# Emptying PSUM banks through ScalarE and adding them to the output by accumulating DMAs, instead of adding on VectorE

## The chip, the cores and the metric

The kernel runs on one core of one Trainium2 chip. The metric is the device time of one execution in microseconds (us), as the median of several runs. Engines are named as in the profile: PE is TensorE (PEld its weight loads), DVE is VectorE, ACT is ScalarE, POOL is GpSimd and SP is SyncE.

## The reference

The input x is 2048 rows of 576 numbers in float32. All is float32.

```python
xn = layernorm(x)                       # over the 576 columns, eps 1e-5
out = x + A(xn, wqkv, wo) + B(xn, w1, w2)

# A: attention, 32 heads of 18; row s sees rows s, s-2, ..., s-14 (masked below 0)
q, k, v = split(xn @ wqkv)              # wqkv 576 x 1728
A = softmax(q . k[s - 2j] / sqrt(18)) @ v[s - 2j], heads joined, @ wo   # wo 576 x 576

# B: a dense layer with relu
B = relu(xn @ w1) @ w2                  # w1 576 x 4608, w2 4608 x 576
```

## The kernel before

The rows are split by parity into two phases (`ph`, `NPH` = 2), since the attention's stride of 2 never mixes them. A phase has eight row tiles of 128 rows (`NI`), which B takes in pairs, four groups (`tb`) of 256 rows. The 4608 inner columns of B are 36 blocks of 128, taken in 12 chunks (`c`, `NCH`) of three (`f`, `C` = 3). One slot is one (ph, c, tb, f), 288 in all, in that order; `slots[n]` names them. The order of all work is written out by hand (a manual schedule): the loop over slots at the end issues, for each, the weight splits that are due (`run_splits`), half of an h product (`h_two`), what `at` has put on this slot (`todo`), the output product (`o_two`, `o_mm` at the two ends), what `late` has put there, and background attention work on DVE (`run_bg`) for as long as a running estimate of DVE's time stays within a margin of PE's.

Each matrix is split into a high part, a copy rounded to the matmul's format by ACT, and a low part, the remainder by DVE (`two` for weights, `h_out` for h, which stands as `hhi` and `hlo`, L651 and L654). A product is then three matmuls: high x high, high x low and low x high. `mm_rows` (L130) runs two matmuls at a time on the upper and lower 64 rows of the array. `h_two` makes the h of two slots in two halves, 28 and 26 matmuls, in PSUM banks called `ph` or `pm`.

`o_two` (L694) adds the three blocks of one chunk for one group into four PSUM banks called `po`: two row tiles (`k`) by two column ranges (`CUT`: 256 and 320 columns). `o_tiles` takes these four banks at f = 0. The first matmul into a bank starts a new sum. At f = 2 `o_out` (L751) empties them. There are just four such banks, so they must be empty before the next group's first output product, half an h product later.

Before the change the sum over chunks lives in SBUF: the x tile itself (`X[ph, i]`, pool `xp`, 11 buffers) is the accumulator, and DVE adds each bank to it:

```python
nc.vector.tensor_tensor(acc[:, cols], PO[k, h], acc[:, cols], op=ALU.add)   # L765
```

After the last chunk SP stores the tile (`store`). The tiles of the second parity are loaded in the last chunk of the first (`XT_STEPS`), normalised and transposed for it (lines L298, L299 and L304 make `xn` on ACT; `make_xt_rows` with L355 and L356 copies the transposes `xT` out of PSUM on ACT, four operations a tile). At some slots `qkv_tile` makes q, k and v in `pm` banks, and ACT copies them out (L472 to L474). The second parity begins at slot 144.

Of the kernel before, what the change touches and what calls it, by code (L numbers as in the profile page):

```python
# [10 lines left out]
F32 = mybir.dt.float32  # L11
F32R = mybir.dt.float32r
AF = mybir.ActivationFunctionType
ALU = mybir.AluOpType
# [4 lines left out]
P = 128  # L19
NPH = 2  # L20
NI = 8
NTB = 4
# [4 lines left out]
C = 3  # L27
# [16 lines left out]
FIRST = 4  # L44
# [14 lines left out]
def tile_body(ctx: ExitStack, tc: tile.TileContext, x, wqkv, wo, w1, w2, out):  # L59
    nc = tc.nc  # L60
    S, D = x.shape
# [4 lines left out]
    NCH = NF // C  # L66
# [3 lines left out]
    CUT = (slice(0, 256), slice(256, D))  # L70
# [6 lines left out]
    pool = lambda name, bufs, **k: ctx.enter_context(tc.tile_pool(name=name, bufs=bufs, **k))  # L77
# [5 lines left out]
        pool(name, 1).tile([P, words], F32, name=name)  # L83

    consts = pool("consts", 1)
    xp = pool("xp", 11)
    xtp = pool("xtp", NTB)
    qop = pool("qop", 1)
    kp = pool("kp", 1)
# [31 lines left out]
    o_v = out.rearrange("(p i two) d -> two i p d", i=NI, two=NPH)  # L121


    t = {"pe": 0.0, "dve": 0.0}
# [2 lines left out]
        nc.tensor.matmul(o, l, r, start=start, stop=stop)  # L127
        t["pe"] += n / 2400.0 + 0.002

    def mm_rows(runs, behind=None):  # L130


        if behind is not None:
            tc.add_manual_dep(nc.tensor.nop().ins, behind.ins.name, SYNC, reason="PSUM banks change rows")
        for pair in zip(*runs, strict=True):
            for z, (o, l, r, start, stop, n) in zip((slice(0, 64), slice(64, P)), pair):
                ins = nc.tensor.matmul(o, l[z], r[z], start=start, stop=stop)  # L137
            t["pe"] += pair[0][5] * 17 / 16 / 2400.0 + 0.001
        return ins

    def dve(n):
        t["dve"] += (n + 70) / 960.0
# [113 lines left out]
    X, XT, XN, MR = {}, {}, {}, {}  # L256
# [187 lines left out]
    def qkv_tile(ph, u, i):  # L444
# [19 lines left out]
        if not second:  # L464
            for h in range(2):
                PQ[h] = ps_m.tile([P, 3, UD], F32, name="pm")
            PQ[2] = mm_rows((run(0, LOWER_MORE), run(1, UPPER_MORE)))
            return
        mm_rows((run(1, LOWER), run(0, UPPER)), PQ[2])
        for h in range(2):  # L470
            j, pq = i - 1 + h, PQ.pop(h)
# [92 lines left out]
    def run_bg(margin):  # L564

        ran = False
        while bg and t["dve"] + bg[0][0] / 960.0 <= t["pe"] + margin and not (ran and bg[0][0] == 0):
            n, f, a = bg.popleft()
            f(*a)
            if n:  # L570
                ran = True
                dve(n)
# [48 lines left out]
    def wo_run(ph, i, h, terms, upper):  # L621

        r, d = OT[ph, i]
        row = [r[:, j] for j in range(KT)] + [r[:, KT] if upper else d[:, KT]] + [d[:, j] for j in range(KT + 1)]
        return [(row[a], WO[ph][b][:, CUT[h]]) for a, b in terms]


    slots = [(ph, c, tb, f) for ph in range(NPH) for c in range(NCH) for tb in range(NTB) for f in range(C)]
    H, PO = {}, {}
# [59 lines left out]
    def o_tiles(n):  # L689
        for h, c in enumerate(CUT):  # L690
            for k in range(2):
                PO[k, h] = ps_o.tile([P, 512], F32, name="po")[:, 0 : c.stop - c.start]

    def o_two(n):  # L694


        ph, c, tb, f = slots[n]
        hi, lo = H.pop(n)
        w = W2[ph, c, f]
        with_wo = c == WO_CHUNK and f == C - 1  # L700
        if f == 0:
            o_tiles(n)

        def run(k, h, upper):
            cs, first = slice(k * P, (k + 1) * P), k == upper
            z = [(l[:, cs], w[:, b, W2CUT[h]]) for l, b in ((hi, 0), (hi, 1), (lo, 0))]
            if with_wo:
                more = wo_run(ph, 2 * tb + k, h, (UPPER_MORE if upper else LOWER_MORE) if first else (UPPER if upper else LOWER), upper)
                z = z + more
            return [  # L710
                (PO[k, h], l, r, f == 0 and first and j == 0, f == C - 1 and not first and j == len(z) - 1, CUT[h].stop - CUT[h].start)
                for j, (l, r) in enumerate(z)
            ]

        for j in range(4):
            k, h = divmod(j, 2)
            behind = PB[j - 2] if j > 1 else PB[3] if j == 0 and f else None
            PB[j] = mm_rows((run(k, h, False), run(1 - k, h, True)), behind)
        if with_wo:
            for k in range(2):  # L720
                OT.pop((ph, 2 * tb + k))
        o_out(n, rows=True)

    PB = [None] * 4

    def o_mm(n, out=True, which=range(2)):
        ph, c, tb, f = slots[n]
        hi, lo = H[n]
        w = W2[ph, c, f]
        end = n == len(slots) - 1  # L730
        if f == 0 and 0 in which:
            o_tiles(n)
        for k in which:
            cs = slice(k * P, (k + 1) * P)
            terms = [(j, l, b, h) for j, (l, b) in enumerate(((hi, 0), (hi, 1), (lo, 0))) for h in range(2)]
            if end:
                terms.sort(key=lambda z: -z[3])
            for j, l, b, h in terms:
                mm(
                    PO[k, h], l[:, cs], w[:, b, W2CUT[h]],  # L740
                    f == 0 and j == 0, f == C - 1 and j == 2, D2,
                )
        if 1 in which:
            H.pop(n)
        if out:
            o_out(n, which)

    def store(ph, i):
        nc.sync.dma_start(o_v[ph, i], X[ph, i])

    def o_out(n, which=range(2), rows=False):  # L751
        ph, c, tb, f = slots[n]
        if f < C - 1:
            return
        end = n == len(slots) - 1
        t["dve"] = max(t["dve"], t["pe"] - 0.4)
        order = [(k, h) for k in which for h in range(2)]
        if rows:
            order.sort(key=lambda z: z[1])
        elif end:  # L760
            order.sort(key=lambda z: (z[0], -z[1]))
        for k, h in order:
            i = 2 * tb + k
            acc, cols = X[ph, i], CUT[h]
            nc.vector.tensor_tensor(acc[:, cols], PO[k, h], acc[:, cols], op=ALU.add)  # L765
            dve(cols.stop - cols.start)
            if end and k:
                (nc.scalar if h else nc.sync).dma_start(o_v[ph, i][:, cols], acc[:, cols])
            elif end and h == 0:
                store(ph, i)  # L770
            elif c == NCH - 1 and h == 1 and not end:
                at(n + 1, store, ph, i)


    todo = {}

    def at(n, f, *a):
        todo.setdefault(n, []).append((f, a))
# [3 lines left out]
    def late(n, f, *a):  # L782
        todo_late.setdefault(n, []).append((f, a))
# [5 lines left out]
    for ph in range(NPH):  # L789
        b = ph * SPP  # L790
        for c in range(NCH):
            for f in range(C):
                s = b + c * SPC + f
                first = ph == c == 0
# [12 lines left out]
        for i in range(NI):  # L807
            z = b + WO_CHUNK * SPC + C - 1
# [36 lines left out]
    both, x_low, w_low, last = TERMS[0:4], TERMS[4:8], TERMS[9:13], [TERMS[8], TERMS[13]]  # L845
# [61 lines left out]
    h4[0]()  # L907
    h4[1]()
    o_out(2, (0,))
    x4 = make_xt(0, 4, parts=True)  # L910
    for f in x4[:3]:
# [11 lines left out]
        (late if k else at)(z, {"stats": stats, "norm": norm, "xt": make_xt}[op], 0, *a)  # L923
    for tb in range(NTB):
        late((8, 8, 9, 7)[tb], twin, tb)
    def margin(n):

        odd, qkv = n % 2 == 0, n + 1 in qkv_slots
        if n + 1 in busy_m | bounded and not qkv:
            return 1.4  # L930
        due = sum(z[0] <= n + 1 for z in (*staged, *tasks))
        if slots[n][3] == 1:
            return (1.8 if odd else 2.7 + 2.4 * qkv) - 0.8 * due + 1.6 * (odd and qkv)
        return (2.5 if odd else 3.5 + 2.4 * qkv) - 0.8 * due + 1.6 * (odd and qkv)
# [6 lines left out]
    for n in range(FIRST, len(slots)):  # L941
        if n == ROW0:
            AHEAD["n"] = 4
        run_splits(n)
        g = n - n % 2 + LAG
        if n < ROW0:
            h_mm(n + LAG)
        elif g < len(slots):
            h_two(g, n % 2 == 1)
        for f, a in todo.pop(n, []):  # L950
            f(*a)
        if ROW0 - 1 <= n < len(slots) - C:
            o_two(n)
        else:
            o_mm(n)
        for f, a in todo_late.pop(n, []):
            f(*a)
        run_bg(margin(n))
# [27 lines left out]
```

## Time and profile before

| what | value |
|---|---|
| time, median of 3 runs | 1143.41 us (1143.14 to 1143.69) |
| span of the profiled execution, first to last instruction | 1141.6 us |
| the three runs themselves | 1143.69, 1143.41, 1143.14 us |
| busy share of PE, DVE, ACT, POOL | 99%, 70%, 27%, 5% |
| granted clock of PE | 1.000 |
| DMA traffic | 83.60 MB, mean 73 GB/s |

The profile is of one execution; its span leaves out what lies around the first and last instruction. Its own time is not listed apart from the three runs, which lie 1.5 to 2.1 us above the span. A group's row reads: line, engine, operation, output and inputs, shapes, count, busy us, mean ns of one, idle time of the engine ahead of them and what ended it. A row of the timeline reads: start, us, engine, line, operation, count, and in brackets how long the engine was idle before it and on what. A row of the waits reads: who waited for whom, us in total, times, longest. In the timeline consecutive operations of one kind are merged, and a matmul's end is modelled.

### The profile page before, as it was taken

How to read it: one execution, taken by the hardware profiler on the slowest of the kernel's cores; microseconds unless marked ns; L12 is line 12 of the kernel's file. 1: busy time of each engine (PE TensorE's matmuls, PEld its weight loads, DVE VectorE, ACT ScalarE, POOL GpSimd, SP SyncE). 2: the span in 40 equal slices, each digit the busy share in tenths (PEclk: the TensorE clock that was granted, in tenths of full speed). 3: DMA queues.
4: the chain of work that ended last, by engine and by line, in shares of the span. 5: the costliest groups of instructions: out<-in, count | busy, mean ns of one | idle time of the engine just before them, and what ended most of it. 6: DMA issues, size and time to landing. Idle time of an engine off the chain costs nothing.

```text
span 1141.6 us, 38695 instructions
## 1 busy us (share of the span) xinstructions
PE 1134.5 (99%) x17224; PEld 1128.4 (99%) x17224; DVE 802.1 (70%) x1522; ACT 303.0 (27%) x854; POOL 57.1 (5%) x84
## 2 busy tenths in 40 slices
PE   8999999999999999999999999999999999999998
PEld 8999999999999999999999999999999999999998
DVE  7415886887788689854674179868868887896433
ACT  4412222222232212322462122222222312222110
POOL 2400000000000000000110000000000000010000
PEclk9999999999999999999999999999999999999999
DMA  6303212130330312622633033032221304136002
GB/s 192 109 2 94 71 47 67 48 98 6 97 98 13 104 33 50 175 57 63 157 122 98 2 101 88 23 85 63 63 59 47 107 2 114 45 81 152 13 2 84
DMA packets 118855, 83.60 MB, mean 73 GB/s; under 512 B 33201, under 2 KB 102449, under 8 KB 118689
## 3 DMA queue, kind: packets, MB, share of 16 engines
q1 hardware_dynamic: 118256, 80.67, 25.6%
q8 instruction: 135, 2.21, 0.8%
q10 hardware_dynamic: 432, 0.46, 0.1%
q14 instruction: 32, 0.25, 0.1%
HBM read 64.95 MB, written 7.96 MB: 64 GB/s over the span
## 4 chain that ended last, share of the span: by engine, by line
PE 96%; issue 2%; DVE 1%; ACT 0%; DMA 0%; DVEq 0%; POOL 0%; ACTq 0%
PE po L137 41%; PE pm L137 28%; PE ph L137 24%; PE ph L127 1%; PE po L127 1%; PE pm L317 0%; DVE pr L544 0%; DMA x<-in_x 0%; PE pm L369 0%; DVE xn L613 0%; PE pm L127 0%; DVE hlo L654 0%; DVE x L765 0%; ACT xT L322 0%; DVE xn L614 0%
## 5 line engine op out<-in xcount | busy, mean ns | idle before, releaser
L137 PE MATMUL po<-w2t,hhi 64*128 64x256 f32 (+1 forms) x4448 | 444.8, 290 | 0.0
L137 PEld LDWEIGHTS po<-w2t,hhi 64*128 64x128 f32 x4448 | 356.1, 184 | 0.6
L137 PE MATMUL po<-w2t,hlo 64*128 64x256 f32 (+1 forms) x2224 | 331.2, 287 | 0.0
L137 PE MATMUL ph<-xT,w1t 64*128 64x256 f32 x4806 | 305.5, 273 | 0.3 <-DVE hlo L654 0.2
L137 PEld LDWEIGHTS ph<-xT,w1t 64*128 64x128 f32 x4806 | 293.7, 184 | 1.5 <-DVE hlo L654 1.1
L765 DVE TENSOR_TENSOR x<-po,x 128x320 f32<-128x320 f32 (+1 forms) x384 | 149.6, 449 | 149.4 <-PE po L137 146.8
L137 PEld LDWEIGHTS po<-w2t,hlo 64*128 64x128 f32 x2224 | 217.2, 184 | 0.0
L651 ACT ACTIVATE hhi<-ph 128x256 fp32r<-128x256 f32 x187 | 62.1, 382 | 496.8 <-PE ph L137 484.6
L137 PE MATMUL pm<-wq,xT 64*128 64x432 f32 x1728 | 178.8, 354 | 0.0
L137 PE MATMUL pm<-xT,w1t 64*128 64x256 f32 x2700 | 170.6, 273 | 0.0
L137 PEld LDWEIGHTS pm<-xT,w1t 64*128 64x128 f32 x2700 | 164.5, 184 | 0.0
L137 PEld LDWEIGHTS pm<-wq,xT 64*128 64x128 f32 x1728 | 160.0, 184 | 2.9
L654 DVE SCALAR_TENSOR_TENSOR hlo<-ph,hhi 128x256 fp32r<-128x256 f32 x187 | 70.8, 418 | 129.6 <-ACT hhi L651 129.5
L651 ACT ACTIVATE hhi<-pm 128x256 fp32r<-128x256 f32 x101 | 33.3, 381 | 214.1 <-PE pm L137 214.1
L505 DVE TENSOR_TENSOR pr<-qo,k 128x1152 f32<-128x1152 f32 x64 | 85.6, 1348 | 0.0
L508 DVE TENSOR_REDUCE lg<-pr 128x64 f32<-128x1152 f32 x64 | 85.3, 1342 | 0.0
L537 DVE TENSOR_TENSOR pr<-lg,v 128x1152 f32<-128x1152 f32 x64 | 85.0, 1348 | 0.3
L544 DVE TENSOR_TENSOR pr<-pr 128x288 f32<-128x288 f32 (+1 forms) x128 | 70.1, 600 | 0.1
L654 DVE SCALAR_TENSOR_TENSOR hlo<-pm,hhi 128x256 fp32r<-128x256 f32 x101 | 38.2, 418 | 32.9 <-ACT hhi L651 32.1
L170 ACT ACTIVATE w2t<-st 128x256 fp32r<-128x256 f32 (+1 forms) x144 | 56.3, 445 | 7.1 <-PE po L137 3.9
L174 DVE TENSOR_TENSOR w2t<-st,w2t 128x256 fp32r<-128x256 f32 (+1 forms) x142 | 57.9, 448 | 0.1
L174 DVE TENSOR_TENSOR w1t<-st,w1t 128x640 fp32r<-128x640 f32 x68 | 55.6, 817 | 2.4 <-ACT w1t L170 2.2
(99 smaller groups left out, 689.8 us busy)
## 6 DMA issues: line engine op xcount, KB each, us to landing
st<-in_w SPq DMA_DIRECT2D x72, 288.0 KB, 3.3
st<-in_w SPq DMA_DIRECT2D x72, 256.0 KB, 3.1
st<-in_wqkv SPq DMA_DIRECT2D x32, 216.0 KB, 3.0
st<-in_w SPq DMA_DIRECT2D x144, 32.0 KB, 2.8
out<-x SPq DMA_DIRECT2D x15, 288.0 KB, 2.4
x<-in_x SPq DMA_DIRECT2D x14, 288.0 KB, 4.4
k<-k SPq DMA_DIRECT2D x8, 441.0 KB, 3.9
v<-v SPq DMA_DIRECT2D x8, 441.0 KB, 4.7
```

The lines of the kernel that those rows point to most:

```text
L127: nc.tensor.matmul(o, l, r, start=start, stop=stop)
L137: ins = nc.tensor.matmul(o, l[z], r[z], start=start, stop=stop)
L170: nc.scalar.activation(hi, src, AF.Copy)
L174: nc.vector.tensor_tensor(lo, src, f32(hi), op=ALU.subtract)
L505: nc.vector.tensor_tensor(pr[i], q, window(k, i), op=ALU.mult)
L508: nc.vector.tensor_reduce(lg[:, i], pr.pop(i).rearrange(heads, d=Dh), axis=AX.X, op=ALU.add)
L537: nc.vector.tensor_tensor(pr[i].rearrange(heads, d=Dh), e, window(v, i).rearrange(heads, d=Dh), op=ALU.mult)
L544: nc.vector.tensor_tensor(o, z[:, 0:n], z[:, n : 2 * n], op=ALU.add)
L651: nc.scalar.activation(hi, pt, AF.Relu)
L654: nc.vector.scalar_tensor_tensor(lo, pt, 0.0, f32(hi), op0=ALU.max, op1=ALU.subtract)
L765: nc.vector.tensor_tensor(acc[:, cols], PO[k, h], acc[:, cols], op=ALU.add)
```

## The change

The sum over chunks moves from SBUF to the output tensor in DRAM. `o_out` copies each bank by ACT into a staging tile `ev` (new pool `evp`, 3 buffers; `xp` goes from 11 to 8), and when both column ranges of a row tile are there, GpSimd issues a DMA that adds the tile to the output (`accum_op=ALU.add`). In the first chunk the output has no sum yet. For the first parity DVE adds x and the bank into `ev`, which SP stores plainly. For the second parity (`seeded`) ACT writes x into the four banks ahead of the first matmul, which then does not start a new sum, and `ev` is again stored plainly. In the last group of the kernel DVE adds the banks to tiles that were loaded back from the output (`last_sums`, issued at the end of the group's first slot), and these are stored in its stead. In `o_out` the estimate of DVE's time is now brought up to PE's only where DVE still adds.

```diff
-    xp = pool("xp", 11)
+    xp = pool("xp", 8)
+    evp = pool("evp", 3)
...
-                ins = nc.tensor.matmul(o, l[z], r[z], start=start, stop=stop)
+                ins = nc.tensor.matmul(o, l[z], r[z], start=start, stop=stop, skip_group_check=seeded)
...
                 PO[k, h] = ps_o.tile([P, 512], F32, name="po")[:, 0 : c.stop - c.start]
+                if seeded(n):
+                    nc.scalar.activation(PO[k, h], X[1, 2 * slots[n][2] + k][:, c], AF.Copy)
+
+    def seeded(n):
+        return slots[n][0] == 1 and slots[n][1] == 0
...
-                (PO[k, h], l, r, f == 0 and first and j == 0, ...)
+                (PO[k, h], l, r, f == 0 and first and j == 0 and not seeded(n), ...)
...
-    def store(ph, i):
-        nc.sync.dma_start(o_v[ph, i], X[ph, i])
...
-        t["dve"] = max(t["dve"], t["pe"] - 0.4)
+        last = ph == NPH - 1 and c == NCH - 1 and tb == NTB - 1
+        if c == 0 or last:
+            t["dve"] = max(t["dve"], t["pe"] - 0.4)
...
-            acc, cols = X[ph, i], CUT[h]
-            nc.vector.tensor_tensor(acc[:, cols], PO[k, h], acc[:, cols], op=ALU.add)
-            dve(cols.stop - cols.start)
-            if end and k:
-                (nc.scalar if h else nc.sync).dma_start(o_v[ph, i][:, cols], acc[:, cols])
-            elif end and h == 0:
-                store(ph, i)
-            elif c == NCH - 1 and h == 1 and not end:
-                at(n + 1, store, ph, i)
+            cols = CUT[h]
+            if last:
+                acc = EV[k]
+                nc.vector.tensor_tensor(acc[:, cols], PO[k, h], acc[:, cols], op=ALU.add)
+                dve(cols.stop - cols.start)
+                if k:
+                    (nc.scalar if h else nc.sync).dma_start(o_v[ph, i][:, cols], acc[:, cols])
+                elif h == 0:
+                    nc.sync.dma_start(o_v[ph, i], acc)
+                continue
+            if k not in EV:
+                EV[k] = evp.tile([P, D], F32, name="ev")
+                EVN[k] = 0
+            acc = EV[k]
+            if c == 0 and not seeded(n):
+                nc.vector.tensor_tensor(acc[:, cols], PO[k, h], X[ph, i][:, cols], op=ALU.add)
+                dve(cols.stop - cols.start)
+            else:
+                nc.scalar.activation(acc[:, cols], PO[k, h], AF.Copy)
+            EVN[k] += 1
+            if EVN[k] == 2:
+                del EV[k]
+                if c == 0:
+                    at(max(n + 1, FIRST), nc.sync.dma_start, o_v[ph, i], acc)
+                else:
+                    nc.gpsimd.dma_start(o_v[ph, i], acc, accum_op=ALU.add)
...
+    def last_sums():
+        for k in range(2):
+            EV[k] = evp.tile([P, D], F32, name="ev")
+            nc.sync.dma_start(EV[k], o_v[NPH - 1, NI - 2 + k])
...
+    late(len(slots) - C, last_sums)
```

The order of PE's instructions is the same in both kernels. Of the 384 evictions by DVE 20 stay with it; 364 become copies by ACT, and 16 writes of x into banks are added there. GpSimd issues 174 accumulating transfers, and SP 16 plain stores of `ev` besides the last tiles'.

More of the change, by code (lines that the diff above doesn't have):

```diff
@@ L128, in mm, with mm_rows @@
         t["pe"] += n / 2400.0 + 0.002
-    def mm_rows(runs, behind=None):
+    def mm_rows(runs, behind=None, seeded=False):
         if behind is not None:
@@ L710, in run @@
             return [
-                (PO[k, h], l, r, f == 0 and first and j == 0, f == C - 1 and not first and j == len(z) - 1, CUT[h].stop - CUT[h].start)
+                (PO[k, h], l, r, f == 0 and first and j == 0 and not seeded(n), f == C - 1 and not first and j == len(z) - 1, CUT[h].stop - CUT[h].start)
                 for j, (l, r) in enumerate(z)
@@ L717, in o_two @@
             behind = PB[j - 2] if j > 1 else PB[3] if j == 0 and f else None
-            PB[j] = mm_rows((run(k, h, False), run(1 - k, h, True)), behind)
+            PB[j] = mm_rows((run(k, h, False), run(1 - k, h, True)), behind, seeded(n))
         if with_wo:
@@ L763, in o_out @@
             i = 2 * tb + k
-            acc, cols = X[ph, i], CUT[h]
-            nc.vector.tensor_tensor(acc[:, cols], PO[k, h], acc[:, cols], op=ALU.add)
-            dve(cols.stop - cols.start)
-            if end and k:
-                (nc.scalar if h else nc.sync).dma_start(o_v[ph, i][:, cols], acc[:, cols])
-            elif end and h == 0:
-                store(ph, i)
-            elif c == NCH - 1 and h == 1 and not end:
-                at(n + 1, store, ph, i)
+            cols = CUT[h]
[13 more added lines that the diff above has]
+            if c == 0 and not seeded(n):
+                assert ph == 0
+                nc.vector.tensor_tensor(acc[:, cols], PO[k, h], X[ph, i][:, cols], op=ALU.add)
[9 more added lines that the diff above has]
+                    nc.gpsimd.dma_start(o_v[ph, i], acc, accum_op=ALU.add)
+    EV, EVN = {}, {}
+    def last_sums():
+        for k in range(2):
+            EV[k] = evp.tile([P, D], F32, name="ev")
+            nc.sync.dma_start(EV[k], o_v[NPH - 1, NI - 2 + k])
     todo = {}
```

## The prediction

> **What bounds the kernel now.** I read the page's engine rows first, then the chain, then TensorE's own waits, then the timeline round the points that the change touches.
>
> ```profile
> span 1141.6 us, 38695 instructions
> PE 1134.5 (99%) x17224; PEld 1128.4 (99%) x17224; DVE 802.1 (70%) x1522; ACT 303.0 (27%) x854; POOL 57.1 (5%) x84
> PE 96%; issue 2%; DVE 1%; ACT 0%; DMA 0%; DVEq 0%; POOL 0%; ACTq 0%
> PEld ph L137 <- DVE hlo L654: 1.1, 3, 0.4
> ```
>
> TensorE (PE) is busy for all but 7.1 us (1141.6 - 1134.5), and the chain is PE's. In its steady part it waits for VectorE 1.1 us in three places, and for the eviction of a PSUM bank nowhere. So nothing that the change takes off VectorE (DVE) can come back as more than those few us, while each new wait of PE is paid in full.
>
> How a group of banks changes hands now (a group is two row tiles, 9.2 us of PE work outside the qkv slots):
>
> ```profile
> 407.29 1.55 DVE L765 TENSOR_TENSOR x<-po,x 128x256 f32<-128x256 f32 x4 [0.56 <-PE po L137]
> 407.52 1.64 PE L137 MATMUL ph<-xT,w1t 64*128 64x256 f32 x26
> 409.00 0.39 PE L137 MATMUL po<-w2t,hhi 64*128 64x256 f32 x4
> 409.20 0.66 ACT L651 ACTIVATE hhi<-ph 128x256 fp32r<-128x256 f32 x2 [5.52 <-PE ph L137]
> 416.50 1.55 DVE L765 TENSOR_TENSOR x<-po,x 128x256 f32<-128x256 f32 x4
> ```
>
> DVE empties four banks between 407.29 and 408.84. PE returns to them at 409.00, since half of an h product (26 matmuls) lies between: that product is the cover.
>
> **Staging on ScalarE (ACT).** Of 384 evictions 364 move: DVE keeps 16 of the first chunk and 4 at the end.
>
> ```profile
> L765 DVE TENSOR_TENSOR x<-po,x 128x320 f32<-128x320 f32 (+1 forms) x384 | 149.6, 449 | 149.4 <-PE po L137 146.8 <-PE po L127 2.6
> L651 ACT ACTIVATE hhi<-ph 128x256 fp32r<-128x256 f32 x187 | 62.1, 382 | 496.8 <-PE ph L137 484.6 <-PE ph L127 12.2
> L612 ACT ACTIVATE k<-pm 128x320 fp32r<-128x320 f32 x16 | 6.2, 444 | 23.8 <-issue 23.8
> DVE hlo L654 <- ACT hhi L651: 161.6, 91, 10.7
> ```
>
> DVE loses 149.6 x 364/384 = 142 us of work that PE never waited for: worth nothing. The planner fills the room with attention work brought forward, up to the same margin ahead of hlo, which today mostly stands ready and waits for hhi (161.6 us): nothing either. ACT gains 182 x 0.382 + 182 x 0.444 = 150 us and comes to 40% of the span. Two hhi of 0.382 take 0.66 together, so one ACT operation starts about 0.10 before the one ahead ends. Four evictions then hold ACT for 0.28 + 0.28 + 0.34 + 0.34 = 1.24 us; the 256-column pair is out after 0.66, the 320-column pair after 1.34. From 407.29 that is 407.95 and 408.63, for banks that PE wants at 409.00 and, the second pair, 0.35 later: hidden by 1.05 and 0.72, and ACT is free at 408.53, before hhi at 409.20. Where the q, k and v copies stand ahead, ACT is free before DVE's eviction begins:
>
> ```profile
> 93.23 0.79 ACT L170 ACTIVATE w1t<-st 128x640 fp32r<-128x640 f32 x1
> 93.34 1.55 DVE L765 TENSOR_TENSOR x<-po,x 128x256 f32<-128x256 f32 x4 [2.51 <-PE po L137]
> ```
>
> So I take nothing for the 364 copies. Were the cover gone, each 0.1 us too late would cost some 9 us over about 90 groups.
>
> **Writing x into the banks.** This adds a wait that PE did not have. At slots 144, 147, 150 and 153 (second parity, first chunk, first step of each group) ACT must write four banks before `o_two` may start. The writes stand in ACT's queue behind that slot's splits, hhi, transposed-x copies and the evictions of the group before; all of PE's work is queued behind its wait. The rows now, by slot:
>
> ```profile
> 578.65 0.76 ACT L170 ACTIVATE w2t<-st 128x256 fp32r<-128x256 f32 x2
> 580.19 0.36 PE L137 MATMUL po<-w2t,hhi 64*128 64x256 f32 x1
> 580.47 0.44 ACT L355 ACTIVATE xT<-pm 128x320 fp32r<-128x320 f32 x1 [1.05 <-PE pm L369]
> 581.22 0.22 ACT L356 ACTIVATE xT<-pm 64x64 fp32r<-64x64 f32 x1
> ...
> 589.37 0.26 ACT L304 ACTIVATE xn<-xn 128x64 f32<-128x64 f32 x1
> 590.30 0.66 ACT L651 ACTIVATE hhi<-ph 128x256 fp32r<-128x256 f32 x2 [0.68 <-PE ph L137]
> 590.34 0.36 PE L137 MATMUL po<-w2t,hhi 64*128 64x256 f32 x1
> ...
> 597.80 1.02 ACT L170 ACTIVATE wq<-st 128x432 fp32r<-128x432 f32 x2
> 598.38 1.55 DVE L765 TENSOR_TENSOR x<-po,x 128x256 f32<-128x256 f32 x4
> 600.19 0.47 PE L137 MATMUL po<-w2t,hhi 64*128 64x256 f32 x4
> ...
> 605.62 0.78 ACT L170 ACTIVATE w2t<-st 128x256 fp32r<-128x256 f32 x2
> 607.78 1.55 DVE L765 TENSOR_TENSOR x<-po,x 128x256 f32<-128x256 f32 x4 [1.65 <-PE po L137]
> 609.49 0.40 PE L137 MATMUL po<-w2t,hhi 64*128 64x256 f32 x4
> ```
>
> No row shows ACT writing PSUM. The bounds are the copies of the same widths out of PSUM (0.382, 0.444) and, SBUF to SBUF, this slot's w2t pair (0.76, against 0.382 + 0.444 - 0.10 = 0.73 for reads of PSUM); they differ little and I take the PSUM ones. The last of four writes then lands 1.34 after the first starts, and PE can run its first 0.35 us on the 256-column banks meanwhile. ACT's steps (durations less 0.10 while others follow):
>
> - Slot 144: evictions where w2t now starts, 578.65 + 1.24 = 579.89; w2t 0.66, 580.55; four xT copies 0.85 (580.47 to 581.32 in the rows), 581.40; writes down at 582.74. PE wanted the banks at 580.19: 582.74 - 0.35 - 580.19 = 2.2 us.
> - Slot 147: evictions behind the norm's last copy, from 589.53, 590.77; hhi 0.56; xT 0.85, 592.18; down at 593.52. Wanted at 590.34: 2.8.
> - Slot 150: evictions from 598.38, 599.62; one wq 0.46, 600.08; down at 601.42. Wanted at 600.19: 0.9.
> - Slot 153: evictions from 607.78, 609.02; wq 0.46 and w2t 0.68, 610.16; hhi 0.56, 610.72; down at 612.06. Wanted at 609.49: 2.2.
>
> Together 8.1 us. A low end: the splits and the evictions of 144 and 147 hidden, 6.7. A high end: no overlap of ACT's operations and evictions at DVE's 1.55, some 1.2 more at each, 13.
>
> **GpSimd's transfers.** 174 accumulating transfers of 288 KB appear, 51 MB to be read, and as much of the output read and written again, against 83.6 MB now; 16 plain stores stay on SyncE (SP), eight of them new at the start, where the queue has time.
>
> ```profile
> out<-x SPq DMA_DIRECT2D x15, 288.0 KB, 2.4
> x<-in_x SPq DMA_DIRECT2D x14, 288.0 KB, 4.4
> DMA to landing us min/median/max: 2.1/2.4/4.7
> q1 hardware_dynamic: 118256, 80.67, 25.6%
> ACT wq L170 <- DMA st<-in_wqkv: 5.1, 5, 1.8
> ```
>
> No row shows an accumulating transfer. At least it is a store, 2.4; at most the slowest store and a median store's time again for reading the output, 4.7 + 2.4 = 7.1. I take 4.1, nearer to the store, as most of it is a store's path. Its buffer (three for two tiles a group) is wanted again when the next group's second copy starts, 416.50 + 0.28 - (407.29 + 1.00) = 8.5 us after the first tile is staged: covered by 1.4 even at 7.1. GpSimd itself is 5% busy; nm, rstd and the qo copies may stand 1 to 2 us behind a transfer's issue, and all have a slot or more in hand: nothing. The queues are a quarter busy; ACT's waits for staged weights may grow, of which none reaches PE today: 0, with up to 6 us kept for the range.
>
> **The end.** The last group's sums so far come back from the output. Its second tile's load must wait for the buffer of the preceding group's first tile.
>
> ```profile
> 1131.12 1.55 DVE L765 TENSOR_TENSOR x<-po,x 128x256 f32<-128x256 f32 x4 [3.10 <-PE po L137]
> 1137.60 0.28 PE L127 MATMUL po<-w2t,hlo 128*128 128x256 f32 x1
> ```
>
> Staged at 1131.12 + 1.00 = 1132.1; accumulated 4.1 later; loaded back in 3.4 (the mean of 2.4 and 4.4): 1139.6. DVE's last two additions would else start near 1137.6: 2.0 us more, between 0 (2.4 + 2.4) and 6 (7.1 + 4.4). The Trainium skill, "DMA: Bandwidth & Descriptors", section "Anatomy of one DMA — SWDGE (gpsimd) path", gives a GpSimd transfer 2.0 us and its bytes over 436 GB/s; as an estimate 2.7 us here, by which this term would be 0.6 and the time 1152.1.
>
> **Sum.** 0 + 8.1 + 2.0 = 10.1 us. The profiled execution would span 1151.7; the median lies 1.8 above the span (1143.4 - 1141.6), so 1153.5 us.
>
> **Rivals.**
> - Faster: the writes of x are hidden, and PE also loses idle time. Of its 7.1 us, 3.7 lie behind its last matmul (1137.60 + 0.28 against 1141.6), so 3.4 are left to win: 1140.0 at best, 1142.3 if only the 1.1 us of waits go. It decides only if ACT reaches its writes 2 us before my steps; for it speaks that ACT is 27% busy, against it that hhi and xT wait for PE's own work of the same slot. 0.05.
> - Nothing measurable (within 0.2%, 2.3 us, about what a measurement of this kernel can tell): part of the change's words does not come true, and PE's first matmul does not wait for the writes, with the end hidden: 1143 to 1145. The program has such a wait ahead of each of these matmuls. 0.05.
> - Late weights: the traffic, more than doubled, holds split operands back, and the 5.1 us that ACT waits for wq, with the like for w1 and w2, become 15; PE gets half of it or all: 1153.5 + 7 = 1160, or 1168. For it: ACT's waits are there already. Against: none costs PE anything now. 0.13.
> - Late buffers: an accumulating transfer takes over 8.5 us and ACT's second copy waits in each of some 90 groups. The first 1.05 us are covered; each us beyond costs 90. At 10.5 us it gives 1153 + 85 = 1240. For it: if an operation of DVE kept GpSimd from writing descriptors, each of the long ones below would add 1.35 us, and four on top of 4.1 reach 9.5. Against: they are not back to back everywhere, DVE being 70% busy. 0.07. The Trainium skill, "SBUF — State Buffer", section "SBUF: two separate sides", has GpSimd locked out in this way while DVE runs in a two-port mode; no row here shows it.
>
> ```profile
> L505 DVE TENSOR_TENSOR pr<-qo,k 128x1152 f32<-128x1152 f32 x64 | 85.6, 1348 | 0.0
> ```
>
> **How the numbers follow.** My own case has 0.70 and gives 1153.5, from 1150 (6.7 and 0) to 1162 (13 and 6 are unlikely together). The range 1149 to 1167 adds most of the late weights; it leaves out the two cases below it (0.10), the late buffers and the worst of the late weights above (0.10). Faster 0.05, same 0.05, slower 0.90.
>
> **What would show it.** In the profile after: PE waiting for ACT's line of the x writes four times between 575 and 615, 2 to 3 us each but for the third; no wait of PE for the staged copies elsewhere; DVE near 660 us and ACT near 460; PE's steady groups unchanged at 9.2 us; the last additions waiting for a load of the output. I am wrong if PE's waits there come to under 4 us, if PE waits for staged copies in the steady part, or if ACT waits for GpSimd's transfers.

## The result, and the profile after

The changed kernel took 1171.89 us, the median of four runs (1168.23 to 1177.96), against 1143.29 us before on the same chip: a ratio on record of 1.0257, with a 95% interval of 1.0227 to 1.0286 (the two medians alone give 1.0250). It is 28.6 us slower. The forecast was 1153.5 us, 10.1 us slower, with a range up to 1167. The sign was right, the size was not. The profiled execution took 1171.29 us with a span of 1169.5.

From the page of the changed kernel, the engines, the queues, the groups that the change added, and three rows of the DMA issues (the last column is the median from issue to landing):

```profile
span 1169.5 us, 39110 instructions
PE 1147.1 (98%) x17224; PEld 1138.1 (97%) x17224; DVE 665.6 (57%) x1158; ACT 424.7 (36%) x1234; POOL 211.1 (18%) x258
...
q0 software_dynamic: 25056, 51.33, 31.1%
q1 hardware_dynamic: 118832, 81.85, 24.5%
...
L796 POOL DMA_DIRECT2D out<-ev x174 | 153.3, 1033 | 866.9 <-ACT ev L789 841.0
L789 ACT ACTIVATE ev<-po 128x256 f32<-128x256 f32 (+1 forms) x364 | 121.0, 416 | 223.4 <-PE po L138 222.4
...
out<-ev POOLq DMA_DIRECT2D x174, 288.0 KB, 5.8
st<-in_w SPq DMA_DIRECT2D x72, 288.0 KB, 4.9
```

The copies cost what was forecast (416 ns each, and DVE falls to 665.6 us). The transfers did not: they land after 5.8 us, and a row tile of weights, which landed after 3.3 us before the change, now takes 4.9. Before the change the same row read:

```profile
st<-in_w SPq DMA_DIRECT2D x72, 288.0 KB, 3.3
```

The waits of the changed kernel (who for whom: us in total, times, longest):

```profile
ACT k L599 <- DMA xn<-words: 11.2, 3, 5.5
PE po L138 <- ACT k L599: 6.5, 2, 3.4
PE po L138 <- ACT po L695: 4.6, 3, 1.9
DVE ev L773 <- DMA ev<-out: 2.8, 1, 2.8
ACT ev L789 <- DMA out<-ev: 1.0, 2, 0.9
```

The third and fourth rows were forecast: PE waits for the writes of x (L695), and the last additions for the reloaded output. The second was not. At two slots PE waits for the split of the attention's output (`wo_split`, L599), which waits for a load of turned words (`xn<-words`).

Both kernels run the same 17224 matmuls in the same order, so the start of the n-th in one trace minus its start in the other gives PE's delay at each point. Read so, the 27.9 us by which the spans differ (1169.5 - 1141.6) arise in these places:

| place | us |
|---|---|
| slots 122 and 266, wait for the words (slot 264 with 1.0 included) | 5.0 + 6.3 |
| slot 143, wait behind a load of transposed x | 2.1 |
| slots 144, 147, 150, 153, writes of x | 3.6 + 4.2 + 1.0 + 2.3 = 11.1 |
| all other steps together, two gains of 0.6 near 512 and 1076 us included | 0.8 |
| behind the last matmul (6.4 against 3.7) | 2.7 |

The delays are longer than the waits, because the clock joins in. Windows of the changed kernel's trace, in pairs of 3.41 us (the columns are busy us and counts of PE, PEld, DVE, ACT, POOL, then the granted clock, the DMA engines' busy share, GB/s; a packet's whole time is counted in the window in which it starts, so a share can pass 1.00):

```profile
480.77:484.18 3.41, 0.12 (x2) 0.12 (x4) 0.14 (x1) 0.74 (x1) 0.00 (x0) 1.00 0.79 147
484.18:487.59 3.41, 3.41 (x32) 3.41 (x34) 0.85 (x2) 0.00 (x0) 0.00 (x0) 0.50 0.68 183
...
600.24:603.65 3.41, 1.47 (x23) 1.21 (x21) 1.98 (x6) 3.41 (x13) 0.07 (x1) 1.00 0.55 187
603.65:607.06 3.41, 3.41 (x28) 3.24 (x28) 0.00 (x0) 0.12 (x1) 0.00 (x0) 0.50 0.16 51
```

A window in which PE did little is followed by one at half clock, in which PE gets 1.7 us (half of 3.41) less done. This comes four times (484, 590, 604 and 1068 us): 6.8 us. Without it the writes of x cost 11.1 - 3.4 = 7.7 us and the words 7.9.

Why are the words late? Windows ahead of slot 122, first before the change, then after:

```profile
471.00:474.00 3.00, 3.00 (x54) 3.00 (x52) 3.00 (x10) 1.32 (x4) 0.00 (x0) 1.00 0.70 194
474.00:477.00 3.00, 3.00 (x54) 3.00 (x54) 3.00 (x5) 0.00 (x0) 0.00 (x0) 1.00 0.90 237
477.00:480.00 3.00, 3.00 (x54) 3.00 (x52) 0.82 (x3) 1.12 (x3) 0.00 (x0) 1.00 0.58 94
```

```profile
471.00:474.00 3.00, 3.00 (x54) 3.00 (x52) 1.37 (x4) 2.54 (x8) 0.65 (x2) 1.00 1.01 196
474.00:477.00 3.00, 3.00 (x54) 3.00 (x52) 1.26 (x3) 0.05 (x1) 1.11 (x2) 1.00 0.83 145
477.00:480.00 3.00, 3.00 (x54) 3.00 (x54) 0.76 (x2) 0.66 (x2) 0.00 (x0) 1.00 1.09 265
480.00:483.00 3.00, 0.69 (x13) 0.49 (x9) 0.00 (x0) 0.00 (x0) 0.00 (x0) 1.00 0.94 209
```

The DMA engines were 0.58 to 0.90 busy there and are now about full. But the traces also allow another reading. From the timelines, SP's issue of the load and the split of a weight (L170 before, L171 after), first before, then after:

```profile
473.57 0.38 SPq L405 DMA_DIRECT2D xn<-words  x1
471.55 0.78 ACT L170 ACTIVATE w2t<-st 128x256 fp32r<-128x256 f32 x2
```

```profile
476.63 0.45 SPq L406 DMA_DIRECT2D xn<-words  x1
473.25 0.80 ACT L171 ACTIVATE w2t<-st 128x256 fp32r<-128x256 f32 x2
```

The load is issued 3 us later. ACT's evictions now stand ahead of that split, so the staging buffer could come free late, and SP's in-order queue hold the words back behind a load into it. So two theories stood open: the **traffic** of the accumulating transfers, and the **queue** of ACT.

### The profile page after: what moved, and what is told of

It reads as the page before. It is cut to its first block, busy times and chain, and to the rows that moved or that the text cites. A ratio compares the mean times of both kernels' runs of the same rounds, so it can differ in the third digit from the quotient of the medians.

```text
span 1169.5 us, 39110 instructions
## 1 busy us (share of the span) xinstructions
PE 1147.1 (98%) x17224; PEld 1138.1 (97%) x17224; DVE 665.6 (57%) x1158; ACT 424.7 (36%) x1234; POOL 211.1 (18%) x258
## 3 DMA queue, kind: packets, MB, share of 16 engines
q0 software_dynamic: 25056, 51.33, 31.1%
HBM read 65.54 MB, written 59.87 MB: 107 GB/s over the span
## 4 chain that ended last, share of the span: by engine, by line
PE 82%; issue 10%; ACT 2%; DMA 2%; DVE 2%; POOL 1%; SPq 1%; POOLq 0%; DVEq 0%; ACTq 0%
PE po L138 34%; PE pm L138 25%; PE ph L138 20%; POOL out L796 1%; PE ph L128 1%; PE po L128 1%; ACT ev L789 1%; DMA xT<-words 0%; DMA xn<-words 0%; DVE pr L538 0%; DVE pr L545 0%; DMA out<-ev 0%; DMA ev<-out 0%; PE pm L318 0%; ACT xn L299 0%
## 5 line engine op out<-in xcount | busy, mean ns | idle before, releaser
L138 PE MATMUL po<-w2t,hhi 64*128 64x256 f32 (+1 forms) x4448 | 450.4, 292 | 4.8 <-ACT po L695 4.6
L138 PEld LDWEIGHTS po<-w2t,hhi 64*128 64x128 f32 x4448 | 360.7, 185 | 7.4 <-ACT po L695 6.1
L138 PE MATMUL po<-w2t,hlo 64*128 64x256 f32 (+1 forms) x2224 | 335.3, 288 | 0.7 <-DVE hlo L655 0.7
L796 POOL DMA_DIRECT2D out<-ev x174 | 153.3, 1033 | 866.9 <-ACT ev L789 841.0
L138 PEld LDWEIGHTS po<-w2t,hlo 64*128 64x128 f32 x2224 | 221.3, 185 | 0.9 <-DVE hlo L655 0.9
L789 ACT ACTIVATE ev<-po 128x256 f32<-128x256 f32 (+1 forms) x364 | 121.0, 416 | 223.4 <-PE po L138 222.4
```

The lines of the kernel that those rows point to most:

```text
L789: nc.scalar.activation(acc[:, cols], PO[k, h], AF.Copy)
L796: nc.gpsimd.dma_start(o_v[ph, i], acc, accum_op=ALU.add)
```

## The experiments

**First set: the writes of x, and traffic against queue.** The writes undone:

```diff
     def seeded(n):
-        return slots[n][0] == 1 and slots[n][1] == 0
+        return False
...
-                assert ph == 0
```

> The second parity's first chunk is summed as the first parity's is: its banks start empty, and VectorE adds x while it evicts them; the rest of the change stays. Theory (each write of x holds TensorE up, and two of the four waits also bring a stretch of 3.4 us at half clock): TensorE's delay of 3.59 + 4.18 + 0.98 + 2.35 = 11.1 us at slots 144 to 153 goes, both dips of the granted clock near 590 and 604 us with it, and the kernel takes 1161 us (1159.5 to 1162.5). Rival (the waits are those of a chip that has other work late there, and the writes only show it): another wait stands at the same slots, and the gain is under 4 us, 1168 or more.

Measured: 1159.58 us (1159.23 to 1163.08), 12.3 us less than the changed kernel. PE's delay at slots 144 to 153 is gone, with both dips near 590 and 604. The theory holds: the writes and the clock behind them cost about what the matmul starts said. Other places shifted by 1 to 2 us in the profiled run, so the agreement is no closer than that.

All transfers cut to one row:

```diff
-    nc.gpsimd.dma_start(o_v[ph, i], acc, accum_op=ALU.add)
+    nc.gpsimd.dma_start(o_v[ph, i][0:1], acc[0:1], accum_op=ALU.add)
```

> GpSimd's transfers carry one row of 128 instead of the whole tile, so that all but one row of the later chunks' sums is left out of the output; every instruction of ScalarE, VectorE and TensorE stays, and the traffic of 52 MB is gone. Theory of the traffic (the accumulating transfers slow the loads that bring back the turned words at slots 122 and 266): the two delays of about 5 us there go, the 1.7 us at slot 143 too, and the kernel takes 1159 to 1161 us. Theory of the queue (ScalarE's copies stand ahead of the split of a weight, the staging buffer comes free late, and SyncE's in-order queue issues the words' load late): both delays stay at 4.5 to 5.5 us, and the kernel takes 1169 to 1172 us.

Measured: 1160.13 us (1153.84 to 1160.45). From its timelines, and then from its waits:

```profile
473.72 0.38 SPq L406 DMA_DIRECT2D xn<-words  x1
473.34 0.80 ACT L171 ACTIVATE w2t<-st 128x256 fp32r<-128x256 f32 x2
```

```profile
PE po L138 <- ACT po L695: 4.7, 3, 2.0
```

The split of the weight is as late as in the changed kernel (473.34), yet SP issues the load at 473.72, as before the change, and PE waits for the writes of x alone. The delays at slots 122, 266 and 143 are gone. The traffic theory holds, the queue theory does not. That the time lies in the theory's range is partly luck: by the matmul starts of the profiled run, slots 122, 266 and 143 and the end cost some 15 us less than in the changed kernel, more than the theory had, and some 5 us came back in the steady part of the second parity, by the loss that the last section shows. The fastest of the four runs took 1153.84 us.

DVE in ACT's place, with the traffic kept:

```diff
-        if c == 0 or last:
+        if c == 0 or last or True:
             t["dve"] = max(t["dve"], t["pe"] - 0.4)
...
+            elif True:
+                nc.vector.tensor_copy(out=acc[:, cols], in_=PO[k, h])
+                dve(cols.stop - cols.start)
             else:
                 nc.scalar.activation(acc[:, cols], PO[k, h], AF.Copy)
```

The first line keeps the planner's estimate of DVE's time as it was before the change.

> VectorE copies the banks to the staging tiles instead of ScalarE, with VectorE's time in the planner's account as before the change; GpSimd's accumulating transfers and the writes of x stay. Theory of the queue: ScalarE's split is in its old place, both delays of 5 us at slots 122 and 266 go, and with the writes of x left in the kernel takes 1160 to 1163 us. Theory of the traffic: both delays stay and the kernel takes 1170 to 1174 us.

Measured: 1176.28 us (1173.97 to 1182.24). ACT is back at 309.2 us and both waits stay:

```profile
PE po L138 <- ACT k L599: 4.4, 2, 2.6
```

The time lies above both theories' ranges, some 4 us above the changed kernel. In the profile PE now also waits for DVE's copies (3.3 us) and its weight loads for splits of weights (3.6 us).

DVE in ACT's place in two groups only (the same two edits, with `n in (119, 263)` in place of `True`):

> Of the banks' copies only the eight of two groups, those that end in slots 119 and 263, go from ScalarE to VectorE; all else is the changed kernel. Theory of the queue: those eight copies stand ahead of the weight's split which holds up the load of the turned words; with them gone both waits (3.3 and 3.6 us) go and with the waits the two stretches at half clock (1.7 us each), and the kernel takes 1161 to 1163 us. Theory of the traffic: nothing changes, 1170 to 1173 us.

Measured: 1176.12 us (1169.06 to 1180.11). From its timelines:

```profile
477.15 0.46 SPq L406 DMA_DIRECT2D xn<-words  x1
472.79 0.78 ACT L171 ACTIVATE w2t<-st 128x256 fp32r<-128x256 f32 x2 [0.98 <-DMA st<-in_w]
484.74 0.74 ACT L599 ACTIVATE k<-xn 128x640 fp32r<-128x640 f32 x1 [6.40 <-DMA xn<-words]
```

Without the evictions ahead of it the split comes only 0.46 us earlier (it now waits for its weight), and the load is as late as ever. That ends the queue theory, which had been my own first reading of the traces. The time is 3 us above the traffic theory's range; in the profiled run about 5 us are again the loss that the last section shows.

**Second set: what in the traffic, where, and what the parts add up to.** The transfers store instead of adding:

```diff
-    nc.gpsimd.dma_start(o_v[ph, i], acc, accum_op=ALU.add)
+    nc.gpsimd.dma_start(o_v[ph, i], acc)
```

> GpSimd's transfers store the tile instead of adding it, so that the output holds only the last chunk's sums; the bytes, the instructions and the waits stay. In the changed kernel 51.33 MB of accumulating transfers took 31.1% of the transfer engines (0.61% a MB) and 81.85 MB of plain ones 24.5% (0.30% a MB). Theory A (it is the adding that makes a byte twice as dear): queue 0 falls to 15 or 16%, the engines are no longer full ahead of slots 122 and 266, those waits fall under 2 us each, no dip of the clock comes there, and with the writes of x left in the kernel takes 1160 to 1165 us. Theory B (the bytes alone, or GpSimd's kind of transfer, fill the engines): the share stays near 31%, the waits stay at about 5 us with their dips, 1169 to 1174 us.

Measured: 1158.94 us (1155.92 to 1160.48). From its page:

```profile
q1 hardware_dynamic: 118832, 81.85, 25.4%
q0 software_dynamic: 13920, 51.33, 12.6%
...
HBM read 65.54 MB, written 59.87 MB: 108 GB/s over the span
...
out<-ev POOLq DMA_DIRECT2D x174, 288.0 KB, 3.0
st<-in_w SPq DMA_DIRECT2D x72, 288.0 KB, 3.5
```

The same row of the changed kernel:

```profile
HBM read 65.54 MB, written 59.87 MB: 107 GB/s over the span
```

The same 51.33 MB take 12.6% of the engines instead of 31.1%, in 80 packets a transfer instead of 144, and land in 3.0 us instead of 5.8. So it is the adding that is dear: 0.61% of the engines a MB against 0.25%. The bytes do not show it: both kernels read 65.54 MB from HBM and write 59.87. The forecast share was 15 or 16%, and the time lies 1 us below the theory's range. The waits fell under 2 us each, as theory A had it (2.5 us in two); one dip stayed at slot 122, which it had not.

Eight of the 174 transfers cut to one row:

```diff
+    r = 1 if n in (116, 119, 260, 263) else P
-    nc.gpsimd.dma_start(o_v[ph, i], acc, accum_op=ALU.add)
+    nc.gpsimd.dma_start(o_v[ph, i][0:r], acc[0:r], accum_op=ALU.add)
```

> Only 8 of the 174 accumulating transfers carry one row of 128 instead of the whole tile (those rows are left out of the output): the transfers of the groups that end in slots 116, 119, 260 and 263, ahead of the load of the turned words that TensorE waits for at slots 122 and 266. Theory of a local crowd: both delays of about 5 us fall under 1 us, the writes of x still cost about 11 us, and the kernel takes 1159 to 1163 us. Rival (the weights have fallen behind over many groups, so that a few transfers make no difference): the delays stay over 3 us each, 1167 us or more.

Measured: 1162.60 us (1159.16 to 1165.57). The window and the wait that answer to those above:

```profile
471.00:474.00 3.00, 3.00 (x56) 3.00 (x54) 1.56 (x5) 2.15 (x8) 0.21 (x1) 1.00 0.44 120
```

```profile
PE po L138 <- ACT k L599: 0.3, 1, 0.3
```

The crowd is local. With eight transfers gone, PE's wait for the split falls from 6.5 to 0.3 us in the profiled run, while the other 166 fill the engines over the span as before (31.3%). The profiled run is the fastest of four; two took over 1165 us, and where they lost it is not known.

Three parts undone together: no writes of x, the eight transfers cut, and the last partial sums loaded earlier:

```diff
-            EV[k] = evp.tile([P, D], F32, name="ev")
+            EV[k] = xp.tile([P, D], F32, name="x")
...
-    late(len(slots) - C, last_sums)
+    late(len(slots) - 2 * C, last_sums)
```

> Three parts of the change undone together: the second parity's first chunk is summed by VectorE as the first parity's; the same 8 transfers carry one row (what they should add is left out of the output); and the last group's partial sums are loaded three slots earlier, into two free tiles of x. ScalarE's staging and 166 of the 174 accumulating transfers stay. If the loss is the sum of these three (11 us of the writes with their dips, 10 us of the two waits with theirs, 2.7 us at the end) and the steady part costs nothing, the kernel takes 1143 to 1146 us, its clock is full until the end, and TensorE's delay against the kernel before is under 1.5 us. Rival (the traffic also costs the steady part something that the dips had covered): 1149 us or more.

Measured: 1148.59 us, ten runs from 1143.89 to 1154.86; the profiled run, 1143.89, has a full clock and a delay of PE of 0.6 us. The edit also dropped the two transfers of the group before the last, so 164 whole ones were left. In the best run the three parts are the whole loss; the median lies 3 us above the theory's range. That is settled below as far as it could be.

The suspected write, 44 times more (the source is a weight scaled by 0 outside the first chunk):

```diff
     def seeded(n):
-        return slots[n][0] == 1 and slots[n][1] == 0
+        return slots[n][0] == 1
```

> The suspected cost, 44 times more: in the second parity every group's banks are written by ScalarE before TensorE adds to them, the first chunk's with x as before, the 44 others with zeros (a weight times 0), in the same four instructions; the output stays what it was. Theory (a write stands between the eviction of a bank and the next group's first matmul, so it is on TensorE's path at every group): 1.0 to 2.5 us a group, 44 to 110 us in all, and where the wait leaves half of a 3.4 us window empty, a dip of 1.7 us more, in a third of the groups or more: 1230 to 1360 us. Rival (the writes are dear only at slots 144 to 153, where ScalarE and VectorE have the new phase's x to prepare): under 0.5 us a group, below 1195 us.

Measured: 1241.65 us in a single run, 70 us above the changed kernel, or 1.6 us for each further group. Of the waits:

```profile
PE po L138 <- ACT po L697: 34.8, 33, 2.0
PEld po L138 <- ACT po L697: 50.2, 79, 2.1
```

The steady groups pay too, though ACT has time there: a write cannot begin before the bank is empty, nor the next product before the write. The waits of weight loads and matmuls overlap; by the larger row a further group waits (50.2 - 6.1) / 44 = 1.0 us (6.1 is that row in the changed kernel). That undercounts. By the matmul starts, the run loses 74 us on the kernel before over the steady groups (645 to 1121 us there): 56 at starts held up by over 0.25 us, among them the later banks of a group, 11 in windows at half clock, and 7 spread over the rest. The windows at half clock, ten against four, followed far fewer groups than a third.

**Third set: staging alone, the spread, and a repair.** No writes of x, all transfers of one row, last sums loaded early:

> ScalarE's staging by itself: the second parity's first chunk is summed by VectorE, all 174 accumulating transfers carry one row (the later chunks' sums are left out of the output), and the last partial sums are loaded three slots earlier. The prediction costed the staging of 364 copies at nothing. If that holds, the kernel takes 1142.3 to 1143.8 us and its runs agree within 1 us, as those of the kernel before do. Rival (ScalarE's copies, standing ahead of its splits and activations, cost the steady part something): over 1145 us.

Measured: 1142.49 us, against 1143.74 for the kernel before, measured beside it: a ratio of 0.9996 (0.9979 to 1.0012). ACT's staging costs nothing that these runs can tell. The profiled run is ahead of the kernel before by the two small waits near 512 and 1076 us, which go with DVE's load. Its runs do not agree within 1 us: three of twelve took 1148 to 1149 us, as did three of 23 of the kernel before.

The three parts again, with the two lost transfers in place and the last sums under a name of their own:

> As the run with three parts undone, but with the two transfers of the group before the last in place, which fell out there: 166 whole accumulating transfers and 8 of one row. The runs of that kernel spread from 1143.9 to 1154.9 us about a median of 1148.6 us, and those at a full granted clock took 1143.9 to 1146.5 us. If the traffic that is left makes the loads late by chance, the spread stays: a median of 1145 to 1151 us with runs up to 1155 us at a clock of 0.997. If the spread was that of the chip on that day, the runs agree within 1 us, at 1143.5 to 1146 us.

Measured: 1149.44 us, ten runs from 1144.67 to 1152.80. The spread stays, and the kernel before, measured beside it, took 1143.74, so it comes with the kernel. The profiled run is again the fastest and shows no delay of PE (-0.4 us at its last matmul; the end behind it takes 5.4 us instead of 3.7). Where the slower runs lose their 4 to 8 us was therefore not seen; that it is the remaining traffic is likely, since the kernel without it has a median of 1142.5, but not shown. The granted clock accounts for some of them at most: of the six runs over 1148 us three had 0.997 and three 0.999 or 1.000.

A whole kernel, with the load of the words moved up instead of the traffic taken away (and no writes of x, last sums early):

```diff
-TURN_STEPS = ((-10, -9, -7, -4), (-7, -5, -3, -1), (-4, -3, 0, 1), (-2, 0, 1, 2))
+TURN_STEPS = ((-10, -9, -7, -4), (-7, -6, -5, -1), (-4, -3, 0, 1), (-2, 0, 1, 2))
```

> A whole kernel that leaves nothing out: the second parity's first chunk is summed by VectorE, the last partial sums are loaded three slots earlier, and of the second turned row's words the store goes one slot earlier and the load two slots, so that on SyncE's in-order queue it stands ahead of the weights of two slots. All 174 accumulating transfers stay. If the wait at slots 122 and 266 is that load's late issue and slow landing, it is issued some 4 to 6 us earlier, both waits (5.9 and 6.6 us with their dips, without the writes of x) fall under 1.5 us, and the kernel takes 1144 to 1149 us. Rival (full engines make whatever stands behind it late instead, the weights or the next words): 1152 us or more.

Measured: 1160.79 us (1158.93 to 1169.49). From its timelines, and then from its waits:

```profile
472.84 0.38 SPq L406 DMA_DIRECT2D xn<-words  x1
473.49 0.78 ACT L171 ACTIVATE w2t<-st 128x256 fp32r<-128x256 f32 x2 [4.74 <-DMA st<-in_w]
500.58 0.74 ACT L599 ACTIVATE k<-xn 128x640 fp32r<-128x640 f32 x1 [7.01 <-DMA xn<-words]
```

```profile
PE po L138 <- ACT k L599: 4.2, 2, 2.5
PE po L138 <- ACT ev L788: 2.0, 2, 1.0
```

The rival holds. The load is issued 3.8 us earlier than in the changed kernel and the wait at slot 122 is gone; but ACT then waits 4.74 us for a weight, its evictions are late for PE at slot 120, and the next words are late at slot 125. Here the new order of the queue only chose who waits. Of PE's delay of 17.7 us at the last matmul about 5 are the loss that the last section shows; without them the time would still be in the rival's range.

## Why the prediction was wrong

- **Staging on ScalarE: 0.** Right. PE waits nowhere in the steady part for a copy, and staging alone measured level with the kernel before. DVE came to 665.6 us (forecast near 660), ACT to 424.7 (near 460: the overlap of its operations, which the working had, was not taken off the 150 us).
- **Writing x: 8.1 us.** Right as a wait: 7.7 without the clock, 1.9, 2.5, 1.0 and 2.3 us at the four slots, against 2.2, 2.8, 0.9 and 2.2. The term that the prediction lacked is 3.4 us of half clock behind two of these waits.
- **GpSimd's transfers: 0.** This step failed. It took an accumulating transfer for little more than a store (4.1 us; 5.8 measured), and it went by "The queues are a quarter busy", a mean over the span, where the stretch ahead of slot 122 was 0.58 to 0.90 busy already, 0.73 in the mean. With an added 0.31 that is over full. It cost 7.9 us of waits for the words, 2.1 at slot 143 and 3.4 of clock. The buffers, which the step did examine, held: ACT waited 1.0 us for them.
- **The end: 2.0 us.** 2.7 measured. The estimate worked out from the Trainium skill, "DMA: Bandwidth & Descriptors", section "Anatomy of one DMA — SWDGE (gpsimd) path", made this term 0.6; its 2.7 us for such a transfer, an estimate too, is near the 3.0 of the plain one here and half the 5.8 of the adding one.
- **The rivals.** "Late weights" (0.13, 1160 to 1168) named the right cause, traffic that holds loads back, with too small a chance and the wrong victim: weights arrived late, yet PE waited for a load that stood behind them on SP's queue. "Late buffers" and the two at or below the time before did not come.

With the sizes measured, the sum reads 7.7 + 7.9 + 2.1 + 2.7 + four dips of 1.7 = 27.2 of the 27.9 us.

## What to carry to other kernels

Before traffic is added, read the DMA engines' busy share in the stretch ahead of each load that the critical engine waits for, not its mean over the span, and price an accumulating transfer by its engine time, here 2.5 times that of a store of the same bytes. A wait on TensorE has a second price: when it leaves a third or more of a 3.4 us window empty, the next window may run at half clock, 1.7 us more. In the one case tried here, moving one load up its queue where the transfer engines were full moved the wait to another.

## What the runs showed of the hardware

**The clock.** All dips of the granted clock to 0.50 lie on one grid of 3.413 us in each run. Nine profiles have such dips before PE's last matmul. Of their windows between the first 10 us and that matmul, each of the nine with over 2 us of idle PE was followed by a slow one, of 41 with 1.1 to 2.0 us idle 24 were, and of those with less only one, which was slow itself. The run with writes in every group shows both outcomes for the same idle time:

```profile
732.30:735.71 3.41, 1.98 (x23) 1.48 (x21) 3.00 (x6) 3.41 (x10) 2.79 (x4) 1.00 0.73 100
735.71:739.12 3.41, 3.41 (x34) 3.41 (x32) 3.41 (x8) 0.92 (x3) 0.00 (x0) 0.50 1.11 262
...
950.70:954.10 3.40, 1.97 (x31) 1.65 (x28) 2.05 (x6) 3.40 (x12) 2.57 (x4) 1.00 0.64 137
954.10:957.50 3.40, 3.40 (x52) 3.22 (x52) 3.40 (x6) 1.86 (x5) 0.32 (x1) 1.00 1.09 224
```

PE is busy 1.98 us in the first window and 1.97 in the third; only the first has a slow successor. The matmuls that start in a window tell the two apart better, 17 against 25 here: of the 25 windows with at most 19 starts 24 were followed by a slow one, of 19 with 20 to 24 starts nine, and of some 3000 with more only one. This is a count over the nine profiles; no run tested it. The Trainium skill, "TensorE: Matmul & The Clock Gate", section "Part 1: The HAM clock gate (the "warmup" mystery)", has this window of 3413 ns, free-running, and the two speeds; the traces agree. Its table has the clock fall after an idle window; here a window idle by less than half sufficed, so the measurement decides.

**Two halves out of step.** In three of the 13 profiles (the two-groups kernel, the one with one-row transfers and the one with the words moved up) PE does 1.3% less in each steady stretch of the second parity at a full clock and with no waits. The same 100 us of the changed kernel, then of the two-groups kernel:

```profile
800.00:900.00 100.00, 100.00 (x1522) 99.92 (x1520) 69.21 (x106) 34.88 (x108) 18.09 (x22) 1.00 0.58 112
```

```profile
800.00:900.00 100.00, 100.00 (x1502) 100.00 (x1501) 68.12 (x103) 35.55 (x110) 17.26 (x21) 1.00 0.56 108
```

`mm_rows` issues its matmuls in pairs, on the upper and lower rows of the array. In these three the distance between the two starts of a pair drifts from 0 to some 57 ns and back, 27 ns in the mean of this stretch; in the others it stays at 3 or 10 ns (but for the run with writes in every group, where it varies too), and the loss comes to about 5 us over the second parity. What sets it off was not found; runs of the kernel before that took 1149 us may be of this kind, but none of them was profiled.
